# Early couples of an attention and feed-forward kernel: the left-over keys' weights in another place, an earlier step, later squares, and an opening by pairs

## The chip, the cores and the metric

The kernel runs on one core of a Trainium2 chip. The metric is the device time of one execution in microseconds (us). All data is float32.

## The reference

An attention block with normalised queries and keys, followed by a feed-forward block on its output:

```python
# q, k, v: (8 batches, 12 heads, 448 rows, 64)
q_n = q / sqrt(mean(q*q, -1) + 1e-6) * g_q          # k_n likewise with g_k
scores = matmul(q_n, k_n.T) / sqrt(64)
attn = exp(scores - max); attn = attn / (sum(attn) + 1e-9)
x = matmul(attn, v)                                  # as (8*448, 12*64) = (3584, 768)
h = x @ w_in                                         # w_in: 768 x 2048
out = (h * sigmoid(h)) @ w_out                       # w_out: 2048 x 768
```

## The kernel before

**Couples.** The heads are taken in pairs, and two pairs (four heads of one batch) make a couple `c`. There are `NC` = 24 couples, three for each batch. The loop is `visit(c)`, then `between(c)`. Every engine works through its own list in the order in which the Python program issues the instructions (the schedule is manual), so what stands earlier in the program stands earlier in the queue of its engine.

**Scores and weights.** Keys lie on partitions: the 448 keys of a pair are three groups of 128 (`j` = 0, 1, 2) and 64 left over (`j` = `LEFT` = 3). `scores(c, j, i)` makes four matmuls for pair `i` of the couple (L712, eight records in the profile) into one of two `sc` buffers in PSUM, and two exponentials on ScalarE (L717), scaled by the roots of the keys' squares, that write the weights to SBUF. For the left-over keys one call does both pairs, 64 keys each. The weights' places are `e[0]`, `e[1]`, `e[2]` by `j`; in the first six couples (`c < GROUP`) odd couples have `other` in place of `e[0]`. The left-over keys' weights have `eleft`, which is the first half of `e[1]`.

**Weighted sums.** `weigh(c, j, step)` multiplies weights by values (L749) into two banks, `av0` and `av1`, by halves of a key group: half of each for one pair and the other half for the other, and the other way around with the other `step`. Each call for a `j` below `LEFT` needs the weights of both pairs. `turn` (L725) is a one-element copy into such a bank at each change of step; TensorE's next weighted sum waits for it. The sums of couple `c` with `j` = 2 and `LEFT` are made in `visit(c + 1)`, between the next couple's first scores. Then VectorE takes the result out of the banks: in couples 1 to 5 by copies (L1419), later by a division (`divide`, L808).

**Sums over keys.** VectorE adds the weights of `j` = 1 to those of `j` = 0 (`add`, L763), and `sum_up(c)` (L783) sums over keys on TensorE: the weights of `j` = 2, then the added ones, then the left-over ones. VectorE inverts the result (L792), and six DMAs spread it over partitions (L799, L801). `divide` uses that one couple later in the early couples.

**Normalising the next couple.** `normalise(c)` returns four pieces: squares of q for pair 0 and pair 1, squares of k for pair 0 and pair 1. A piece is a square on ScalarE (L467), a reduce on VectorE (L468) and then, at once or for both pairs together, a root: a small scaling on VectorE (L492) and a power on GpSimd (L496). For q the rows are then scaled on GpSimd (L511). `visit` runs the pieces as `beside`, at four points. At the end of a couple `transpose_q` (L629) and `transpose_k` (L647) turn the next couple's rows on TensorE, and ScalarE copies them to `qT` (L633) and `kT` (L649).

**The opening.** Before the loop, couple 0 is normalised by `norm` itself: both pairs' q, then both pairs' k, and couple 0's queries are turned pair by pair (L629, L631). In `visit(0)` couple 1 is normalised by `normalise_alone(1)`, whose squares are on VectorE.

**What else runs early.** The weights `w_in` arrive by DMA in pieces and are opened on ScalarE (L100, L101) and rounded on VectorE and GpSimd (L123 to L134); some sums of them are made on VectorE (L854). From couple 3 on, `fill` deals matmuls of the feed-forward block (L902) between the couples; from couple 6 on they fill TensorE between the attention steps. After the last couple the rest of the feed-forward block follows (L1209).

Of the kernel before, what the change touches and what calls it, by code (L numbers as in the profile page):

```python
# [190 lines left out]
def kernel(  # L191
# [176 lines left out]
    with tc.manual_schedule(), tc.tile_pool(  # L368
# [45 lines left out]
        for i in range(2):  # L414
            norm.squares_q(0, first_q, first_squares[i], i)
            norm.root(0, "q", i)
        for i in range(2):
            norm.squares_k(0, place["k0"], first_squares[i], i)
            norm.root(0, "k", i)
            norm.scale(0, first_q, place["q0"], i, nc.vector)  # L420

    def arm():

        r = copy.copy(room)
        r.w_in = copy.copy(room.w_in)
        state = [dict() for _ in pairs]
        return dict(
            tc=tc, nc=nc, z=z, pairs=pairs, room=r, ring=ring, w_out=w_out, ident=ident,
            minus_half=minus_half, gains=gains, out=out,
            own=dict(  # L430
                NC=NC, loads=loads, place=place, norm=norm, spare=spare, ones=ones, first=first,
                second_q=second_q, squares=squares,
            ),
            plain=(state, lambda n: load_pair(state, n)),
        )
# [100 lines left out]
def bounded(  # L536
# [36 lines left out]
    eleft = e[1][:, 0]  # L573
# [35 lines left out]

    def xT(b, c):  # L610
        return sets[b // 2 % 2].rearrange("p (b c s) -> p b c s", b=2, c=z.NW)[:, b % 2, c, :]
# [7 lines left out]

    def transpose_q(c):  # L620

        t = ps.tile([P, 2, BANK], F32, name="sc", bufs=2)
        both = [t[:, i] for i in range(2)]
        if c == 0:
            both[1] = ps.tile([P, BANK], F32, name="av1")
        for i in range(2):
            for j in range(J):
                rows = q_of(c)[0:R, ts(i * J + j, 2 * D)]
                nc.tensor.transpose(both[i][:, ts(j, R)], rows, ident[0:R, 0:R])  # L629
            if c == 0:  # L630
                (nc.scalar.copy, nc.vector.tensor_copy)[i](qT[:, i], both[i][:, 0:S])  # L631
        if c > 0:
            nc.scalar.copy(qT, t[:, :, 0:S])  # L633
        if GROUP - 2 <= c <= GROUP:
            load_q(c + 2)
        elif c > GROUP + 1:
            load_q(c + 1)
# [65 lines left out]
    def scores(c, j, i=None):  # L703
# [12 lines left out]
        for h in range(2):  # L716
            nc.scalar.activation(  # L717
                eleft[:, h] if j == LEFT else weights(c, j)[:, i, h], two[:, h, 0:S], AF.Exp,
                scale=norm.column(c, i, h, j),
            )  # L720
# [6 lines left out]
    def weigh(c, j, step=0):  # L727
# [6 lines left out]
        for i in order:  # L734
# [5 lines left out]
            for h in range(2):  # L740
                if j == LEFT:
                    v, w = place[f"vleft{c % 2}"][rows, ts(h, D)], eleft[rows, h]
# [11 lines left out]
    def add(c, j):  # L754

        def one(i):
            total = weights(c, 0)[:, i]
            if j == LEFT:
                rows = ds(i * D, D)
                total, more = total[rows], eleft[rows]  # L760
            else:
                more = weights(c, j)[:, i]
# [4 lines left out]
    def sum_up(c):  # L767
# [10 lines left out]
        for k, (which, w) in enumerate(terms):  # L778
            if k == len(terms) - 2:
                yield  # L780
            for h in range(2):
                for i in range(2):
# [3 lines left out]
                        eleft[:, h] if which else w()[:, i, h],  # L786
# [53 lines left out]
    def normalise_alone(c):  # L840

        source = raw_of(c)
        for i in range(2):
            norm.squares_q(c, source, scratch[i], i, True)
            norm.root(c, "q", i)
        norm.squares_k(c, place[f"k{c % 2}"], scratch[0], 0, True)
# [550 lines left out]
    def visit(c):  # L1397

        beside = normalise(c + 1) if 0 < c <= GROUP else []
        if c == GROUP:  # L1400
            beside = beside[2:]
        if c < NC:
            scores(c, 0, 0)
        if c == 0:
            normalise_alone(1)
        run_all(beside[0:1])
# [8 lines left out]
        if c > 0:  # L1415
            weigh(c - 1, LEFT - 1, 1)
            if c - 1 < EARLY:
                for i in range(2):
                    nc.vector.tensor_copy(x_of(c - 1, i), sums[i])  # L1419
                run_all(beside[1:2])  # L1420
# [16 lines left out]
        scores(c, 1, 0)  # L1437
        scores(c, 1, 1)
        if c < GROUP:
            run_all(beside[2:3])  # L1440
        weigh(c, 0, 1)
        scores(c, 2, 0)
# [4 lines left out]
        scores(c, 2, 1)  # L1447
        weigh(c, 0, 0)
        run_all(add(c, 1))
# [3 lines left out]
        scores(c, LEFT)  # L1453
# [80 lines left out]
    transpose_q(0)  # L1534
# [229 lines left out]
```

## Time and profile before

| what | value |
|---|---|
| timed runs | 1325.13 us median of 3 (1323.84 to 1328.43) |
| the profiled execution | 1323.7 us, span 1321.9 us |
| granted TensorE clock, mean | 0.998 |
| TensorE busy | 1298.3 us (98%) |
| VectorE busy | 949.2 us (72%) |
| ScalarE busy | 505.2 us (38%) |
| GpSimd busy | 361.5 us (27%) |
| first scores of couples 0 to 6 | 10.25, 24.25, 40.30, 55.84, 75.98, 97.47, 116.46 us |

How to read it: times in the profile count from the start of the span. PE is TensorE's matmuls, PEld its weight loads, DVE VectorE, ACT ScalarE, POOL GpSimd, SPq the queue that issues most DMAs. A row of the timeline gives start, length, engine, line of the kernel, operation, result and operands; several like instructions that follow each other are merged (`x8`). Brackets give the engine's idle time before the row and who ended it. Ends of matmuls are modelled, so TensorE's starts are read rather than its lengths.

### The profile page before, as it was taken

What the parts mean: (1) busy time and instruction counts of PE and PEld (TensorE: products, weight loads), DVE (VectorE), ACT (ScalarE), POOL (GpSimd) and SP (SyncE); (2) the same over time, 40 slices, a digit from 0 to 9 for tenths busy, and PEclk for the clock granted to TensorE, in tenths of its full rate; (3) what the DMA queues carried; (4) which work ended last, traced back from release to release, by engine and by line L of the source; (5) the groups of instructions that cost most, each with busy time, mean ns of one, the idle gap of its engine ahead of it and who ended that gap; (6) DMA issues with size and microseconds to landing.
All of it is one profiled execution on the core that took longest, in us unless ns stands there. A gap on an engine that the chain in (4) does not pass through costs nothing.

```text
span 1321.9 us, 19806 instructions
## 1 busy us (share of the span) xinstructions
PE 1298.3 (98%) x7193; PEld 829.3 (63%) x7193; DVE 949.2 (72%) x1629; ACT 505.2 (38%) x886; POOL 361.5 (27%) x230
## 2 busy tenths in 40 slices
PE   8989999999999999999999999999999999999998
PEld 4433444444444444444444455558999999999998
DVE  6888776776755555855554686698978787878785
ACT  7966656645545545454444253410100000001000
POOL 6756444343334334333420244410000000000000
PEclk9999999999999999999999999999999999999999
DMA  8674337233443444444321367412323232231411
GB/s 232 169 189 110 113 91 209 80 90 91 95 116 91 97 103 107 96 93 117 81 67 67 106 197 259 150 60 76 100 76 106 76 101 90 92 114 63 132 45 39
DMA packets 249439, 144.94 MB, mean 110 GB/s; under 512 B 184292, under 2 KB 233220, under 8 KB 249332
## 3 DMA queue, kind: packets, MB, share of 16 engines
q1 hardware_dynamic: 248672, 142.42, 38.5%
q8 instruction: 59, 0.97, 0.3%
q0 software_dynamic: 352, 0.96, 0.2%
q14 instruction: 48, 0.39, 0.1%
q10 hardware_dynamic: 308, 0.20, 0.1%
HBM read 93.98 MB, written 41.29 MB: 102 GB/s over the span
## 4 chain that ended last, share of the span: by engine, by line
PE 83%; DVE 6%; ACT 4%; DMA 3%; issue 2%; POOL 1%; SPq 1%; ACTq 0%; DVEq 0%; POOLq 0%
PE mm L902 25%; PE alone L1209 23%; PE mm L1209 8%; PE av L749 8%; PE sc L712 7%; PE alone L902 7%; PE alone L1246 2%; PE sc L783 1%; DMA work<-work 1%; DVE work L763 1%; DVE work L792 1%; ACT work L717 1%; PE mm L1246 1%; ACT stage L1040 1%; DMA hidden<-stage 1%
## 5 line engine op out<-in xcount | busy, mean ns | idle before, releaser
L902 PE MATMUL mm<-x,W 128*128 128x448 f32 x612 | 246.7, 546 | 4.7 <-DVE parts L857 2.0
L717 ACT ACTIVATE work<-sc,rms 128x448 f32<-128x448 f32 x324 | 184.8, 634 | 71.9 <-PE sc L712 58.0
L902 PE MATMUL mm<-sums_x,W 128*128 128x448 f32 x480 | 193.4, 543 | 1.5 <-DVE parts L857 1.5
L902 PEld LDWEIGHTS mm<-x,W 128*128 128x128 f32 x612 | 112.3, 190 | 131.1 <-issue 104.3
L712 PE MATMUL sc<-work 64*64 64x448 f32 x1344 | 165.6, 546 | 1.8 <-ACT work L717 1.5
L763 DVE TENSOR_TENSOR work<-work 128x896 f32<-128x896 f32 (+1 forms) x114 | 123.7, 1118 | 50.1 <-PE av L749 49.6
L749 PE MATMUL av<-work,rows 64*64 64x448 f32 x1296 | 154.1, 543 | 3.3 <-ACT av L725 2.2
L902 PEld LDWEIGHTS mm<-sums_x,W 128*128 128x128 f32 x480 | 89.6, 190 | 95.2 <-issue 85.5
L496 POOL TENSOR_TENSOR rms<-rms,minus_half 128x14 f32<-128x14 f32 (+4 forms) x43 | 105.2, 2449 | 149.2 <-DVE rms L492 139.6
L523 POOL DMA_DIRECT2D out_dram<-x x2 | 1.2, 594 | 443.3 <-DVE x L857 443.3
L1209 PE MATMUL alone<-W,rows 128*128 128x192 f32 x610 | 113.0, 326 | 0.0
L749 PEld LDWEIGHTS av<-work,rows 64*64 64x64 f32 x1296 | 57.8, 132 | 75.7 <-issue 35.8
L1209 PEld LDWEIGHTS alone<-W,rows 128*128 128x128 f32 x610 | 101.5, 190 | 0.0
L712 PEld LDWEIGHTS sc<-work 64*64 64x64 f32 x1344 | 53.6, 133 | 74.8 <-ACT work L717 29.2
L922 POOL TENSOR_TENSOR parts<-parts,stage 128x448 f32<-128x448 f32 x31 | 42.1, 1357 | 148.8 <-DVE parts L857 143.1
L688 POOL TENSOR_TENSOR rms<-rms,minus_half 128x28 f32<-128x28 f32 x12 | 57.5, 4794 | 64.1 <-DVE rms L685 57.4
L1209 PE MATMUL alone<-W,work 128*128 128x192 f32 x382 | 72.2, 326 | 0.0
L1040 ACT ACTIVATE stage<-stage 128x896 f32<-128x896 f32 x63 | 57.3, 945 | 23.6 <-DVE stage L857 22.9
L1219 ACT COPY rows<-alone 128x192 f32<-128x192 f32 x33 | 10.5, 319 | 142.1 <-PE alone L1209 78.4
L468 DVE TENSOR_REDUCE rms<-rows 128x8 f32<-128x512 f32 (+2 forms) x56 | 35.9, 640 | 39.1 <-ACT rows L467 37.9
L1209 PEld LDWEIGHTS alone<-W,work 128*128 128x128 f32 x382 | 63.8, 190 | 0.0
L792 DVE RECIPROCAL work<-sc 128x224 f32<-128x224 f32 x38 | 58.6, 1547 | 5.7 <-PE sc L783 5.5
(250 smaller groups left out, 2114.5 us busy)
## 6 DMA issues: line engine op xcount, KB each, us to landing
hidden<-stage SPq DMA_DIRECT2D x63, 448.0 KB, 3.1
work<-hidden SPq DMA_DIRECT2D x21, 1024.0 KB, 5.1
rows<-in_moe_w_out_dram SPq DMA_DIRECT2D x32, 384.0 KB, 3.4
W<-in_moe_w_in_dram SPq DMA_DIRECT2D x22, 512.0 KB, 5.1
work<-work SPq DMA_DIRECT2D x141, 56.0 KB, 2.0
x<-hidden SPq DMA_DIRECT2D x7, 1024.0 KB, 5.6
rows<-in_q_dram SPq DMA_DIRECT2D x96, 56.0 KB, 2.3
rows<-in_k_dram SPq DMA_DIRECT2D x96, 56.0 KB, 2.3
```

The lines of the kernel that those rows point to most:

```text
L496: nc.gpsimd.tensor_tensor(out=t, in0=t, in1=half, op=ALU.pow)
L688: nc.gpsimd.tensor_tensor(out=f, in0=f, in1=minus_half.to_broadcast([P, n]), op=ALU.pow)
L712: nc.tensor.matmul(two[ds(half * D, D), h, 0:S], keys[rows, ts(half, D)], qT[rows, pair, :], start=True, stop=True,)
L717: nc.scalar.activation(eleft[:, h] if j == LEFT else weights(c, j)[:, i, h], two[:, h, 0:S], AF.Exp, scale=norm.column(c, i, h, j),)
L749: nc.tensor.matmul(sums[i][ds(h * D, D), :], v, w, start=(j == 0 and step == 1), stop=(j == LEFT - 1 and step == 1),)
L763: nc.vector.tensor_tensor(out=total, in0=total, in1=more, op=ALU.add)
L792: nc.vector.reciprocal(out=r[0][:, rows], in_=t[:, rows])
L902: nc.tensor.matmul(t, self.left(name, s), self.right(name, s), start=s == ends[0], stop=s == ends[1])
L922: nc.gpsimd.tensor_tensor(out=u2, in0=u2, in1=p5, op=ALU.add)
L1040: nc.scalar.activation(t, t, AF.Silu)
L1209: nc.tensor.matmul(t, x[:, i], y, start=i == ORDER[0], stop=i == ORDER[-1])
L1246: nc.tensor.matmul(o, a[:, 2 * i + m, t], right_one(name, i)[:, m], start=n == 0, stop=n == len(steps) - 1,)
```

## The change

There are four edits, all in the first seven couples.

1. The left-over keys' weights go to `left_weights(c)`. In couples 0 to 5 that is the second half of the place that the next couple's `j` = 0 weights will have, which the couple before used. From couple 6 on it stays the first half of `e[1]`.
2. In couples 0 to 5 `scores(c, LEFT)` is issued one weighted sum sooner, ahead of `add(c, 1)`, `weigh(c, 1, 0)` and, in couples 0 to 2, ahead of the opening of a weight piece.
3. Couple 4 runs its first piece of `normalise` (q, pair 0) together with the second, behind the copies of the last couple's sums. Couple 6 runs its two k pieces one point later each: the first behind the division, the second behind the scores of `j` = 1.
4. The opening goes pair by pair. k's root of pair 0 comes before q's root of pair 1; the scaling and the transposes of pair 1's queries move into `visit(0)`; and couple 0's scores are made for pair 0 with `j` = 0, 1, 2 and then for pair 1 with `j` = 0, 1, 2, all before the first weighted sum. Couple 1's normalising is split by a `yield` after the first half of its q.

```diff
-        for i in range(2):
-            norm.squares_q(0, first_q, first_squares[i], i)
-            norm.root(0, "q", i)
-        for i in range(2):
-            norm.squares_k(0, place["k0"], first_squares[i], i)
-            norm.root(0, "k", i)
-            norm.scale(0, first_q, place["q0"], i, nc.vector)
+        norm.squares_q(0, first_q, first_squares[0], 0)
+        norm.root(0, "q", 0)
+        norm.squares_q(0, first_q, first_squares[1], 1)
+        norm.squares_k(0, place["k0"], first_squares[0], 0)
+        norm.root(0, "k", 0)
+        norm.root(0, "q", 1)
+        norm.scale(0, first_q, place["q0"], 0, nc.vector)
+        norm.squares_k(0, place["k0"], first_squares[1], 1)
+        norm.root(0, "k", 1)
...
+    def left_weights(c):
+
+        return weights(c + 1, 0)[:, 1] if c < GROUP else e[1][:, 0]
...
+    def first_turn(i):
+
+        if i == 0:
+            t = ps.tile([P, 2, BANK], F32, name="sc", bufs=2)[:, 0]
+        else:
+            t = ps.tile([P, BANK], F32, name="av1")
+        transpose_q_half(0, i, t)
+        (nc.scalar.copy, nc.vector.tensor_copy)[i](qT[:, i], t[:, 0:S])
...
             norm.squares_q(c, source, scratch[i], i, True)
             norm.root(c, "q", i)
+            if i == 0:
+                yield
...
         if c == GROUP:
-            beside = beside[2:]
+            beside = [lambda: None] + beside[2:]
         if c < NC:
             scores(c, 0, 0)
         if c == 0:
-            normalise_alone(1)
-        run_all(beside[0:1])
+            alone = normalise_alone(1)
+            next(alone)
+            scores(c, 1, 0)
+            norm.scale(0, own["first_q"], place["q0"], 1, nc.vector)
+            first_turn(1)
+            run(alone)
+            scores(c, 2, 0)
+        if c != GROUP // 2 + 1:
+            run_all(beside[0:1])
...
-                run_all(beside[1:2])
+                run_all(beside[0 if c == GROUP // 2 + 1 else 1 : 2])
...
-        scores(c, 1, 0)
+        if c > 0:
+            scores(c, 1, 0)
         scores(c, 1, 1)
-        if c < GROUP:
+        if c <= GROUP:
             run_all(beside[2:3])
+        if c == 0:
+            scores(c, 2, 1)
         weigh(c, 0, 1)
-        scores(c, 2, 0)
+        if c > 0:
+            scores(c, 2, 0)
         weigh(c, 1, 1)
         turn(0, nc.scalar.copy)
         if c < GROUP:
             run_all(beside[3:4])
-        scores(c, 2, 1)
+        if c > 0:
+            scores(c, 2, 1)
         weigh(c, 0, 0)
+        if c < GROUP:
+            scores(c, LEFT)
         run_all(add(c, 1))
         weigh(c, 1, 0)
         if c < GROUP // 2:
             room.w_in.open()
-        scores(c, LEFT)
+        if c >= GROUP:
+            scores(c, LEFT)
...
     transpose_k(0)
-    transpose_q(0)
+    first_turn(0)
```

More of the change, by code (lines that the diff above doesn't have):

```diff
@@ L431, in arm @@
                 NC=NC, loads=loads, place=place, norm=norm, spare=spare, ones=ones, first=first,
-                second_q=second_q, squares=squares,
+                first_q=first_q, second_q=second_q, squares=squares,
             ),
@@ L571, in bounded @@
     e = [piece(4 * S).rearrange("p (i h s) -> p i h s", i=2, h=2) for _ in range(3)]
-    eleft = e[1][:, 0]
     r = [piece(S) for _ in range(2)]
@@ L618, in bounded, with transpose_q_half @@
     LEFT = z.KEYS
+    def transpose_q_half(c, i, t):
+        for j in range(J):
+            rows = q_of(c)[0:R, ts(i * J + j, 2 * D)]
+            nc.tensor.transpose(t[:, ts(j, R)], rows, ident[0:R, 0:R])
+    def first_turn(i):
[5 more added lines that the diff above has]
+        (nc.scalar.copy, nc.vector.tensor_copy)[i](qT[:, i], t[:, 0:S])
     def transpose_q(c):
         t = ps.tile([P, 2, BANK], F32, name="sc", bufs=2)
-        both = [t[:, i] for i in range(2)]
-        if c == 0:
-            both[1] = ps.tile([P, BANK], F32, name="av1")
         for i in range(2):
[L627 to L633, printed above, removed]
+            transpose_q_half(c, i, t[:, i])
+        nc.scalar.copy(qT, t[:, :, 0:S])
         if GROUP - 2 <= c <= GROUP:
@@ L717, in scores @@
             nc.scalar.activation(
-                eleft[:, h] if j == LEFT else weights(c, j)[:, i, h], two[:, h, 0:S], AF.Exp,
+                left_weights(c)[:, h] if j == LEFT else weights(c, j)[:, i, h], two[:, h, 0:S], AF.Exp,
                 scale=norm.column(c, i, h, j),
@@ L741, in weigh @@
                 if j == LEFT:
-                    v, w = place[f"vleft{c % 2}"][rows, ts(h, D)], eleft[rows, h]
+                    v, w = place[f"vleft{c % 2}"][rows, ts(h, D)], left_weights(c)[rows, h]
                 else:
@@ L759, in one @@
                 rows = ds(i * D, D)
-                total, more = total[rows], eleft[rows]
+                total, more = total[rows], left_weights(c)[rows]
             else:
@@ L785, in sum_up @@
                         ones[:, which + i if which else 0],
-                        eleft[:, h] if which else w()[:, i, h],
+                        left_weights(c)[:, h] if which else w()[:, i, h],
                         start=(k == 0), stop=(k == len(terms) - 1),
```

## The prediction

> **What bounds the kernel now.** I read the page, then the busy time by stretches, then the timeline of the first 160 us.
>
> ```profile
> PE 1298.3 (98%) x7193; PEld 829.3 (63%) x7193; DVE 949.2 (72%) x1629; ACT 505.2 (38%) x886; POOL 361.5 (27%) x230
> ```
>
> TensorE leaves 23.6 us of the 1321.9 us span. The stretches show where (start:end, length, then busy us of PE, PEld, DVE, ACT, POOL, the granted clock, DMA):
>
> ```profile
> 56.00:76.00 20.00, 17.95 (x161) 7.37 (x157) 15.80 (x23) 14.28 (x27) 13.03 (x8) 1.00 0.55 139
> 76.00:97.00 21.00, 19.63 (x161) 8.30 (x161) 17.24 (x27) 14.56 (x27) 11.85 (x7) 1.00 0.76 193
> ...
> 116.00:126.00 10.00, 7.88 (x58) 2.43 (x56) 9.79 (x18) 6.55 (x14) 6.05 (x5) 0.83 0.37 91
> ```
>
> Couple 3 fills 55.84 to 75.98, couple 4 up to 97.47, and couple 6 begins at 116.46. The diff touches nothing after couple 6. From 155 to 700 us TensorE is busy for 538.63 of 545 us, so what the first 130 us win or lose should reach the end almost whole. In couples 1 and 2 (24 to 56 us) TensorE is busy for 31.77 of 32 us.
>
> The timeline (start, length, engine, line, operation; in brackets the idle time before and who ended it) shows the stalls. In the opening, ScalarE's exponentials:
>
> ```profile
> 11.36 4.55 ACT L717 ACTIVATE work<-sc,rms 128x448 f32<-128x448 f32 x8 [2.02 <-PE sc L712]
> 16.20 1.16 ACT L717 ACTIVATE work<-sc,rms 128x448 f32<-128x448 f32 x2 [0.29 <-PE sc L712]
> 17.25 0.17 ACT L725 COPY av<-minus_half 128x1 f32<-128x1 f32 x1
> ```
>
> In couple 3 the left-over keys' exponential waits until VectorE has read e[1], and TensorE's turn of the next keys waits for that exponential:
>
> ```profile
> 68.56 2.10 DVE L763 TENSOR_TENSOR x<-x,work 128x896 f32<-128x896 f32 x2
> ...
> 69.76 1.16 ACT L717 ACTIVATE work<-sc,rms 128x448 f32<-128x448 f32 x2 [3.69 <-DVE x L763]
> ...
> 70.97 0.98 PE L647 MATMUL sc<-ident,rows 128*128 128x128 f32 x7 [2.05 <-ACT work L717]
> ```
>
> In couple 4 TensorE waits for VectorE's copies of the last couple's sums; after it, GpSimd's last scaling of the next queries:
>
> ```profile
> 81.46 1.15 DVE L1419 COPY x<-av 128x448 f32<-128x448 f32 x2
> ...
> 82.14 1.13 PE L749 MATMUL av<-work,rows 64*64 64x448 f32 x6 [0.66 <-DVE x L1419]
> ```
>
> ```profile
> 86.06 1.04 POOL L511 TENSOR_TENSOR x<-x,rms 112x512 f32<-112x512 f32 x1
> ```
>
> In couple 6 it waits for the fence (L725) that stands behind a square of k on ScalarE, runs slowly after that, and waits again, for the division (L808):
>
> ```profile
> 121.67 1.73 PE L749 MATMUL av<-work,rows 64*64 64x448 f32 x8 [1.97 <-ACT av L725]
> 123.16 2.69 PE L712 MATMUL sc<-work 64*64 64x448 f32 x16
> 126.06 1.12 PE L749 MATMUL av<-work,rows 64*64 64x448 f32 x6 [0.21 <-DVE x L808]
> ```
>
> ```profile
> 125.39 1.15 DVE L808 TENSOR_TENSOR x<-av,work 128x448 f32<-128x448 f32 x2
> ```
>
> **The change part by part.** A step of scores or of a weighted sum takes 0.75 us on a full TensorE (starts at 28.52, 30.02 after two of them); a pair of exponentials takes 1.14 (4.55 / 4).
>
> *Opening.* No arithmetic is added or dropped. VectorE takes one small scaling (0.17) more ahead of the first pair's normalising, which moves from 7.44 to 7.6 and ends at 8.3; transposes and copy follow (8.36, 9.0 to 9.53), and the first scores start at 9.6 instead of 10.25, since the second pair's transposes no longer stand before them. GpSimd has k's root second (7.5 + 1.54 = 9.1), in time. The exponentials start 1.11 later (11.36 - 10.25), at 10.7. But now all six pieces come before any weighted sum, because the first weighted sum needs both pairs. The six end at 10.7 + 6 x 1.14 = 17.6; the last scores start when the fourth piece frees its bank (15.3), then two weighted sums (to 17.7), and the fence copy behind them lets TensorE go on at about 18.2. Before, that was 17.48. The rest of the couple is the same full list as before, so couple 1 begins at 24.25 + 0.7. The second pair's normalising (VectorE, 0.69) waits for the third root on GpSimd, 10.7, and its transposes (0.6) fit in TensorE's holes. Behind it VectorE has couple 1's remaining squares, not needed before 19.9. No DMA changes place in SP's queue. **+0.7 us** at 25 us; bounds -0.65 (first score's lead kept) and +0.8.
>
> *Left-over keys.* The 4 matmuls and 2 exponentials move ahead of one weighted sum and, in couples 0 to 2, of the two opening passes of a weight piece (0.70 + 0.69). In couples 1 and 2 TensorE's own list is full, so the order inside it gives nothing: **0**. The passes now run after the exponential; ScalarE's slack before kT (0.69 idle at 22.72, 0.62 at 38.77, 0.61 at 54.31) covers them; without it 1.4 us a couple. In couple 3 the wait for L763 goes: the exponential can run at 66.3 instead of 69.76 and k's turn at 68.86 instead of 70.97. What is late next is the sum over keys (L783), which needs that same L763, done at 70.66: it ends at 72.2 instead of 73.5, and couple 4's scores start at 74.7, 1.3 earlier. Next, couple 4 runs into VectorE: the division at 75.24 waits 2.19 for a DMA (the spread of couple 2's reciprocals), then a weight rounding to 77.9, the reciprocals 77.84 to 80.80, then the copies. None of that moves by an earlier TensorE. So **0** of the 1.3 is kept by itself.
>
> *Couple 4's q squares later.* The reduce and scaling (0.66 between 80.80 and 81.46) go behind the copies: the weighted sum starts at 81.4 instead of 82.14. What goes with them: two squares on ScalarE (0.63 each) now stand between exponentials, still in time (the fence at about 84.4 against 85.52), no DMA (that load is only made for earlier couples), and on GpSimd two roots (1.64) and two scalings (1.04), which follow the reduce. They start at 82.85 instead of 81.64 and end at 82.85 + 5.4 = 88.3, where 87.1 was the end. TensorE is ready for the second half of those queries at 87.4, so now it waits for GpSimd and has its transposes at 88.85, against 89.08 before: **-0.2**; bounds -1.1 (GpSimd in time) and +2.2 (roots of 2.48 and scalings of 1.48, the longest rows for these shapes).
>
> *Couple 6's k squares later.* The fence then follows the first exponential (119.4), and the next four steps of TensorE end at about 122.0 instead of 125.85. But the next weighted sum still needs the division, and VectorE is busy for 9.79 of 10 us there. The division gains only the one reduce that stood before it (0.68 at 124.80): **-0.6**. The second key group's exponentials are then long done, so the 0.6 us wait for the fence before 129.69 shrinks: **-0.4**. The second k reduce goes behind eight sums of 0.62 and k's root with it, to about 135; it is needed at 156.
>
> Against this stands the clock. The idle 119.6 to 121.7 was followed by half clock:
>
> ```profile
> 122.50:123.00 0.50, 0.50 (x8) 0.18 (x4) 0.50 (x2) 0.50 (x2) 0.38 (x2) 0.50 0.67 155
> ```
>
> The granted clock (0.50 here) came down at about 121.75 and was back by 125.2. That cost nothing before, because TensorE had to wait for the division anyway. Now there is one idle gap from 122.0 to about 125.2, 3.2 us. If the clock falls 2.1 us into it, as it did, and stays down 3.4 us, it covers 2.3 us of the work after the restart, which then takes 1.15 longer: **+1.1**; bounds 0 (couple 3's 2.05 us of idling, with the clock at 1.00 after it) and +1.7 (all 3.4 us at half speed). I take +1.1, since this gap is longer than the one that did bring the clock down.
>
> The Trainium skill, "TensorE: Matmul & The Clock Gate" (Part 1, and the table "Why this matters for your kernels"), says that activity is judged in free-running windows of about 3.4 us and that gaps of over about 3 us should be avoided: a rule against this change. Here 2.1 us were enough once and not enough once. By the rule alone this term would be +1.7, an estimate of mine from that page's half rate over one window, and the sum 0.6 higher.
>
> *Sum.* The opening's +0.7 is carried whole by the full couples 1 and 2. In couples 3 and 4 VectorE's chain hangs on a DMA whose issue moves with the program and whose landing also depends on bytes already queued (DMA share 0.76 there); between 0 and +0.7 I take +0.5, nearer to the program. +0.5 - 0.2 - 0.6 - 0.4 + 1.1 = **+0.4 us**. The profiled execution took 1323.7 us (span 1321.9 and 1.8 around it), so 1324.1. The three timed runs have their median 1.4 higher, but one of them (1323.84) at the profile's level; I stay with it. About 0.3%, 4.0 us, is what a measurement of this kernel can tell from no change.
>
> **The rivals.**
>
> *The stalls are gone for good: faster.* If the spread of the reciprocals lands earlier, because couples 0 to 2 send it off sooner, VectorE's chain moves and TensorE keeps its gaps: 2.05 (couple 3), 0.7 (couple 4), 1.97 and, with the clock staying up, 1.9 (three steps from 121.67 took 4.2, not 2.25), together 6.6; less the opening's 0.7 it is 5.9 faster, 1317.8. For it: each edit sits on a bracketed TensorE wait. Against: 75.24 waits for a DMA, and VectorE has 0.2 us free in 116 to 126.
>
> *GpSimd's chain in couple 4 becomes the bound: slower.* Place: the second half of couple 5's queries. Price: TensorE could start them at 87.4. Each microsecond that GpSimd's last scaling ends after 88.5 (88.3 here) costs one. With the longest rows for these shapes the two roots and scalings take 7.9 instead of 5.4 and end at 90.8, +2.2 on the old time; and since TensorE then idles 3.4 us, the clock comes down for another 3.4 us, +1.7. With the opening's 0.5 and the +0.1 of couple 6 (-0.6 - 0.4 + 1.1) that is +4.5, 1328.2. For it: the same root took 1.64 at 44.12 and 2.48 at 46.98. Against: in this couple both took 1.64.
>
> *It doesn't do what it says.* If the left-over keys' exponential still waits, now for the sums that read the last couple's place, couples 3 and 4 stay as they were: 0.5 - 0.6 - 0.4 + 1.1 = +0.6, 1324.3. That place is read last before 56 us (sum of couple 2), ten before couple 3 writes there, so I give it little.
>
> **How the numbers follow.** My sum 0.55, the faster case 0.27, GpSimd's chain 0.13, no effect 0.05. The sum's unknowns (opening -0.65 to +0.8, couple 4 -1.1 to +2.2, clock 0 to +1.7) put it at some 1321.5 to 1327. Half of the faster case lies below its 1317.8, so the range reaches from 1317.8 to 1328.3 and leaves out some 0.13 below and 0.07 above. Over 0.3% faster: most of the faster case and a little of the sum, 0.27. Slower by that: the larger part of GpSimd's case and a tail of the clock's, 0.13. Same: 0.60.
>
> **What would show it.** Right: first exponential at 10.7, couple 1's first scores near 25.0; no wait for L763 before the left-over exponential of couple 3, and k's turn there near 69; in couple 4 the copies straight after the reciprocals, and TensorE waiting for L511 before the second half of the queries; in couple 6 no wait for L725 after the left-over sums, one gap before the weighted sum that follows L808, and a granted clock of 0.50 behind it. Wrong: couple 1 starting before 24.25; the division by couple 2's sums (75.24) well before 74.5; a clock of 1.00 from 122 to 130.

## The result and the profile after

The changed kernel takes 1326.70 us (median of 20 runs, 1324.08 to 1329.03), the kernel before 1324.11 (20 runs, 1322.69 to 1328.43): the ratio is 1.0017 [1.0010, 1.0023]. Run again later, it took 1325.85 against 1324.62, 1.0006 [0.9997, 1.0014]. By these ratios the change costs 2.3 us (1.3 to 3.0) in the first comparison and 0.8 us (-0.4 to 1.9) in the second; the medians lie 2.6 and 1.2 us apart. The forecast was +0.4, and a gain was given more chance than a loss. The profiled executions differ by more, spans of 1325.8 and 1321.9 us, and the two of them alone mislead: two later kernels whose first five couples are those of before began couple 4 at 77.62 and 81.11 us instead of 75.98, and the changed kernel, profiled again, at 75.79 instead of 77.65.

The page's busy times:

```profile
PE 1299.9 (98%) x7193; PEld 830.4 (63%) x7193; DVE 951.7 (72%) x1629; ACT 505.4 (38%) x886; POOL 362.6 (27%) x230
```

TensorE is busy for 1.6 us longer than before and idle for 2.3 us longer (25.9 against 23.6). The busy time by two stretches around couple 6 (columns as in the prediction):

```profile
116.00:126.00 10.00, 9.41 (x71) 3.90 (x71) 9.78 (x14) 8.65 (x17) 3.50 (x6) 1.00 0.27 65
126.00:155.00 29.00, 26.62 (x122) 13.87 (x123) 26.82 (x39) 13.89 (x23) 16.69 (x10) 0.94 0.38 112
```

The stretch from 116 to 126 us has filled up (9.41 of 10 busy, clock 1.00, against 7.88 and 0.83), and the next one has lost more: the granted clock is 0.94 there and TensorE is busy for 26.62 of 29, where it was 28.58 before. VectorE is busy for 26.82 of those 29 (25.30 before). A part of this is only a shift: couple 6 begins at 119.82 instead of 116.46, so the same point of it comes 3.4 us later in these fixed stretches.

The opening in the timeline of after (start, length, engine, line, operation; in brackets the idle time before):

```profile
10.48 2.21 ACT L729 ACTIVATE work<-sc,rms 128x448 f32<-128x448 f32 x4 [1.19 <-PE sc L724]
11.57 0.69 DVE L513 TENSOR_TENSOR rows<-W,rms 112x512 f32<-112x512 f32 x1 [0.60 <-POOL rms L498]
12.32 0.60 PE L629 MATMUL av<-ident,rows 112*128 112x112 f32 x4 [1.24 <-DVE rows L513]
13.93 4.50 ACT L729 ACTIVATE work<-sc,rms 128x448 f32<-128x448 f32 x8 [1.24 <-PE sc L724]
```

The exponentials start 0.9 earlier than before, but stop for 1.24 us after two of the six pieces: the scores of the third stand in TensorE's list behind the turn of the second pair's queries, and these wait for VectorE, which waits for GpSimd's third root. The six end at 18.43 and couple 1 begins at 25.79.

Couple 3, and the division that waits for the spread reciprocals, in after:

```profile
68.04 1.16 ACT L729 ACTIVATE work<-sc,rms 128x448 f32<-128x448 f32 x2 [0.38 <-PE sc L724]
70.44 0.98 PE L659 MATMUL sc<-ident,rows 128*128 128x128 f32 x7
71.41 2.10 DVE L775 TENSOR_TENSOR x<-x,work 128x896 f32<-128x896 f32 x2
72.55 1.59 PE L795 MATMUL mm<-x,ones 128*32 128x448 f32 x5 [1.12 <-DVE x L775]
78.07 1.16 DVE L820 TENSOR_TENSOR x<-x,work 128x448 f32<-128x448 f32 x2 [2.17 <-DMA work<-work]
```

The left-over exponential (68.04) no longer waits for VectorE, and k's turn follows at once. What is late next is the sum over keys (72.55), and the division still waits 2.17 us for its DMA.

Couple 4:

```profile
83.55 1.09 DVE L1440 COPY x<-av 128x448 f32<-128x448 f32 x2
84.17 1.12 PE L761 MATMUL av<-work,rows 64*64 64x448 f32 x6 [0.97 <-DVE x L1440]
89.94 1.90 POOL L513 TENSOR_TENSOR x<-x,rms 112x512 f32<-112x512 f32 x1
91.90 0.60 PE L629 MATMUL sc<-ident,x 112*128 112x112 f32 x4 [1.12 <-POOL x L513]
```

The copies stand directly behind the reciprocals, and TensorE now waits 1.12 us for GpSimd's last scaling, which took 1.90 us where the same line took 1.04 before.

Couple 6, TensorE's timeline and then half a microsecond behind the gap in the stretches (the granted clock is the seventh figure):

```profile
123.64 1.77 PE L724 MATMUL sc<-work 64*64 64x448 f32 x16
128.38 1.48 PE L761 MATMUL av<-work,rows 64*64 64x448 f32 x6 [2.97 <-DVE x L820]
```

```profile
130.00:130.50 0.50, 0.50 (x8) 0.36 (x4) 0.50 (x1) 0.00 (x0) 0.50 (x1) 0.50 0.83 280
```

The fence's wait is gone, and there is one gap of 2.97 us before the weighted sum behind the division, with half the clock behind it. From that weighted sum to the first feed-forward matmul (136.84) it is 8.5 us; before it was 6.9 (126.06 to 132.93).

### The profile page after: what moved, and what is told of

Same layout as the page of the kernel before. It is cut to its first block, busy times and chain, and to the rows that moved or that the text cites. A ratio compares the mean times of both kernels' runs of the same rounds, so it can differ in the third digit from the quotient of the medians.

```text
span 1325.8 us, 19802 instructions
## 1 busy us (share of the span) xinstructions
PE 1299.9 (98%) x7193; PEld 830.4 (63%) x7193; DVE 951.7 (72%) x1629; ACT 505.4 (38%) x886; POOL 362.6 (27%) x230
## 4 chain that ended last, share of the span: by engine, by line
PE 84%; DVE 5%; ACT 4%; DMA 2%; issue 2%; POOL 1%; SPq 1%; ACTq 0%; DVEq 0%; POOLq 0%
PE mm L916 25%; PE alone L1223 22%; PE av L761 8%; PE mm L1223 8%; PE sc L724 7%; PE alone L916 7%; PE alone L1260 2%; PE sc L795 1%; DVE work L775 1%; DVE work L804 1%; ACT work L729 1%; PE mm L1260 1%; DMA work<-work 1%; ACT stage L1054 1%; DMA hidden<-stage 1%
## 5 line engine op out<-in xcount | busy, mean ns | idle before, releaser
L729 ACT ACTIVATE work<-sc,rms 128x448 f32<-128x448 f32 x318 | 181.2, 634 | 68.6 <-PE sc L724 58.6
L775 DVE TENSOR_TENSOR work<-work 128x896 f32<-128x896 f32 (+1 forms) x114 | 123.7, 1118 | 50.7 <-PE av L761 50.1
L1054 ACT ACTIVATE stage<-stage 128x896 f32<-128x896 f32 x63 | 57.3, 945 | 23.2 <-DVE stage L871 22.4
L470 DVE TENSOR_REDUCE rms<-rows 128x8 f32<-128x512 f32 (+2 forms) x56 | 35.9, 640 | 39.3 <-ACT rows L469 38.1
```

Source lines behind the costliest of these rows:

```text
L729: nc.scalar.activation(left_weights(c)[:, h] if j == LEFT else weights(c, j)[:, i, h], two[:, h, 0:S], AF.Exp, scale=norm.column(c, i, h, j),)
L775: nc.vector.tensor_tensor(out=total, in0=total, in1=more, op=ALU.add)
L1054: nc.scalar.activation(t, t, AF.Silu)
```

## The experiments

All times of a run are compared with the kernel before in the same runs. The edits: O the opening, L the left-over keys, Q couple 4's q, K couple 6's k.

**Each edit by itself.** Four kernels, each the kernel before with one part of the change: L is edits 1 and 2 of the list, O is edit 4, Q and K are the two halves of edit 3.

O alone:

> The kernel before with the opening by pairs alone. Theory (the opening loses, and the full couples 1 and 2 carry the loss whole): ScalarE's first exponential near 10.5 us, but a pause before the third pair of them, the first weighted sum near 17.0, couple 1's first scores near 25.8 instead of 24.25, couple 3's near 57.4, and the time 1.5 to 2.8 us longer than before. Rival (the loss is absorbed in couples 3 and 4, where VectorE waits for a DMA): couple 4's weighted sum within 0.5 us of 82.1, the time at most 0.5 us longer. If the opening were not what costs, couple 1 would begin within 0.3 us of 24.25.

Measured 1325.48 against 1323.58 us, 1.0009 [0.9999, 1.0019]; couple 1 begins at 25.45. In its profile couple 3 begins 1.2 us later than before (57.03 against 55.84), couple 4's weighted sum 0.4 later (82.57 against 82.14) and couple 5 0.4 later (97.91 against 97.47). That is what the rival expected of the profile; the time, with its interval, decides between neither.

L alone:

> The kernel before with the left-over keys' edits alone (their place, and one weighted sum sooner). Theory (couple 3's gain of TensorE is taken back by VectorE's chain, which hangs on a DMA): no wait for L763's successor in couple 3, couple 4's first scores 1.1 to 1.3 us earlier (near 74.8), couple 4's first weighted sum still at 82.1, the time within 0.5 us of before. Rival A (the gain is kept): couple 6 begins 1.3 to 2.1 us earlier, the time 1.3 to 2.1 us shorter. Rival B (this edit is what costs, because the opening of weight pieces comes later on ScalarE): couples 1 and 2 longer by some tenths each, the time 1 us longer.

Measured 1324.16 against 1323.58, 1.0000 [0.9990, 1.0011]. In its profile k's turn in couple 3 stands at 68.90 with no wait before it, and couple 4 begins at 74.47 instead of 75.98. Its couple 6 begins 1.4 us earlier than before (115.05 against 116.46), which is what rival A expected; but the time shows no gain, and in a second profile of the same kernel (further down) couple 6 begins at 116.00.

Q alone:

> The kernel before with couple 4's first q piece moved behind the copies, alone. Theory (GpSimd's second scaling becomes what TensorE waits for): copies near 80.8 and the weighted sum near 81.5 instead of 82.1, but the scaling ends 1.2 to 3 us later than 87.1, TensorE's second half of the next queries waits for it, couple 5 begins 0.3 to 1.5 us later than 97.47, and so does the end. Rival (GpSimd is in time): couple 5 begins 0.6 to 1.1 us earlier, the time shorter by as much.

Measured 1324.82 against 1323.58, 1.0003 [0.9993, 1.0012]. In its profile GpSimd's last scaling took 1.84 us instead of 1.04, and couple 5 begins 22.72 us behind the division by couple 2's sums instead of 22.23.

K alone:

> The kernel before with couple 6's k squares later, alone. Theory (the division frees TensorE 0.6 to 1.0 us sooner, but one long gap takes the place of two and the clock falls behind it): weighted sum near 125.3 instead of 126.06, granted clock 0.50 for some 3.4 us after it, the feed-forward matmuls that began at 132.93 begin 0.3 to 0.9 us later, the time 0 to 0.9 us longer. Rival (the clock stays up, or its fall costs nothing): those matmuls 0.6 to 1.4 us earlier, the time shorter by as much.

Measured 1325.66 against 1323.58, 1.0009 [0.9998, 1.0021]. Its couples 1 to 5 are those of before, and yet couple 4 begins at 81.11: the division by couple 1's sums (65.22) came late and long, the left-over exponential with it (72.42), and TensorE waited:

```profile
73.64 1.76 PE L647 MATMUL sc<-ident,rows 128*128 128x128 f32 x7 [3.77 <-ACT work L717]
```

The granted clock was 0.50 from 72.06 to 78.88 us there, as it was not in before. So one profile of one edit cannot price it at a microsecond, nor do the four intervals alone. What follows takes differences inside a profile that repeat from run to run.

**Each edit left out.** The changed kernel without O, without Q, without K:

> The changed kernel with the old opening. Theory (the opening is one of three costs, about 1 us): couple 1 begins between 24.2 and 25.4 us as with the old opening in the runs so far (24.25, 24.25, 25.18, 25.44), against 25.45 and 25.79 with the new one; the time 0.7 to 1.5 us shorter than the changed kernel, so 0.5 to 1.8 us longer than before. Rival (the opening's loss disappears in couple 3's wait for a DMA): the time as the changed kernel's, 2.2 us longer than before.

> The changed kernel with couple 4's first q piece back in its old place. Theory (that edit costs 0.3 to 1.3 us by GpSimd's later scaling): no wait of TensorE for GpSimd's scaling in couple 4 or a shorter one, copies 0.6 us later behind the reciprocals, the time 0.3 to 1.3 us shorter than the changed kernel. Rival (the edit gains its 0.66): the time 0.3 to 0.7 us longer than the changed kernel.

> All edits but couple 6's later k squares. Theory (couple 6's edit costs 0.5 to 1 through the longer gap and the half clock): the fence's wait of 1.97 in couple 6 is back, couple 6 lasts 38.1 to 38.7, and the time is 0.5 to 1 below the unchanged new kernel, about 1 above before (the opening). Rival (couple 6's edit is neutral, the cost lies in the opening and in couple 4): the time is that of the unchanged new kernel.

Measured: without O 1325.23 against 1324.12, 1.0007 [0.9998, 1.0015]; without Q 1326.44 against 1324.12, 1.0013 [1.0004, 1.0021]; without K 1326.24 against 1324.62, 1.0007 [0.9999, 1.0016]. Leaving out any one of the three leaves the kernel slower than before in the median, but two of the three intervals take in 1, so these runs do not say which edit carries the cost. In the profiles the parts come and go as expected: without O couple 1 begins at 24.25; without Q TensorE no longer waits for GpSimd's scaling in couple 4; without K the fence's wait of 1.97 us is back, but couple 6 lasts 39.79 us, longer than the 38.1 to 38.7 expected. The changed kernel again, in the same runs as the last of them:

> The new kernel unchanged, once more, for comparison in the same runs. All theories: 1326.0 to 1327.0; couple 1 begins between 25.4 and 25.8; the gap before the division in couple 6 is 2.9 to 3.5 us with a granted clock of 0.50 behind it; couple 4 begins anywhere between 75 and 79, because the landing of the spread reciprocals differs between executions of the same code.

1325.85 against 1324.62, as told above; couple 1 at 25.56, couple 4 at 75.79, the gap 3.09 us.

**Couple 6: is the half clock a cost?** In the changed kernel, matmuls that nobody reads are put into the gap. The first attempt wrote into a scores bank:

```diff
+    spot = {}
...
-        two = ps.tile([P, 2, BANK], F32, name="sc", bufs=2)
+        two = spot["t"] = ps.tile([P, 2, BANK], F32, name="sc", bufs=2)
...
             run_all(beside[2:3])
+        if c == GROUP:
+            for _ in range(7):
+                nc.tensor.matmul(
+                    spot["t"][:, 0, S:BANK], ident, ident[:, 0 : BANK - S], start=True, stop=True
+                )
```

> The changed kernel with seven small matmuls more (identity by 64 columns of identity, into unused columns of the scores' bank) in couple 6's gap, behind the scores of the second key group; nothing reads their result. Theory (the clock falls because of the one long gap): the gap shrinks to under 1 us, the granted clock stays at 1.00 through the weighted sum behind the division, the feed-forward matmuls of couple 6 begin 4.5 to 7 us after that weighted sum instead of 8.5, the time 1.2 to 2 us shorter than the changed kernel. Rival (the clock's fall is not what costs): the time as the changed kernel's.

1325.99 against 1324.12, 1.0011 [1.0002, 1.0020]. It tells nothing: the seven waited 1.66 us for the exponentials that read the same bank, and the clock still fell. The second attempt writes into a free bank of the feed-forward products:

```diff
+        if c == GROUP:
+            spot = ps_mm.tile([P, BANK], F32, name="mm")
+            for _ in range(12):
+                nc.tensor.matmul(spot[:, 0:P], ident, ident, start=True, stop=True)
```

> All four edits, and in couple 6 twelve small matmuls (identity by identity, their result is read by nobody) into a free bank of the feed-forward products, issued behind the scores of j = 1, where TensorE otherwise idles for 3.0 to 3.5 us until the division. Unlike in the kernel with seven dummies they wait for nothing on ScalarE. Theory (the half clock behind the gap is a cost of its own): TensorE's gap shrinks below 1 us, the clock stays at 1.00 behind the division, the stretch from that weighted sum to the first feed-forward matmul of couple 6 goes from 8.5 back to 6.9 us, couple 6 lasts 37.2 instead of 38.8, and the time is 1.6 us below that of the unchanged new kernel in the same runs. Rival (VectorE's and GpSimd's lists set the end of couple 6): the clock stays up too, but TensorE then waits for the sums of x (L868) or the added weights, couple 6 lasts 38.5 to 39.3, and the time is within 0.5 of the unchanged new kernel.

1326.38 against 1324.62, 1.0013 [1.0004, 1.0021]. TensorE in this kernel, and the same half microsecond as above:

```profile
123.09 2.94 PE L1466 MATMUL mm<-ident 128*128 128x128 f32 x24
126.33 1.12 PE L761 MATMUL av<-work,rows 64*64 64x448 f32 x6 [0.30 <-DVE x L820]
...
138.65 4.78 PE L916 MATMUL mm<-x,W 128*128 128x448 f32 x12 [0.76 <-DVE parts L871]
143.95 1.02 PE L916 MATMUL mm<-sums_x,W 128*128 128x448 f32 x2 [0.52 <-DVE parts L871]
```

```profile
130.00:130.50 0.50, 0.50 (x10) 0.28 (x12) 0.50 (x1) 0.26 (x1) 0.50 (x1) 1.00 0.22 46
```

The gap is filled, the clock stays at 1.00, and the stretch to the first feed-forward matmul is 6.9 us again (126.33 to 133.20). But TensorE then waits 0.76 and 0.52 us for VectorE's sum of products (`parts`, L871), and couple 6 lasts 39.06 us (117.57 to 156.63) instead of 38.84. So in the changed kernel the half clock had no price, though with little to spare: twelve feed-forward matmuls take 4.53 us by their starts (132.93 to 137.46 in before), so after its 24 TensorE could have gone on at 145.9 in after (136.84 + 2 x 4.53, an estimate), and it went on at 146.00 (below). The same twelve matmuls with L and K alone:

> The kernel before with the left-over keys' edit, couple 6's later k squares and the same twelve matmuls in couple 6; the opening and couple 4 as before. Theory (the edits of couple 6 gain 0.6 and 0.4, and the half clock takes that and more back): with the clock at 1.00 couple 6 lasts 37.7 instead of 38.7, and the time is 1.0 below before, the one version that would beat both. Rival (the sums of x become the bound, as when they were moved): couple 6 lasts 38.7 or more and the time is that of before or up to 1 us more.

1325.01 against 1324.62, 1.0002 [0.9994, 1.0011]; clock 1.00, couple 6 38.89. The version that was to beat both does not.

**What does set the end of couple 6?** In 15 of the 18 profiles VectorE's second sum into `parts`. In the kernel before VectorE has these rows behind the division (the one at 125.39 in the prediction), and TensorE waits for the last of them:

```profile
127.03 1.06 DVE L492 TENSOR_SCALAR rms<-rms 128x14 f32<-128x14 f32 x1
128.66 1.60 DVE L854 TENSOR_TENSOR sums_x<-x,sums_x 128x448 f32<-128x448 f32 x1
...
141.82 0.62 DVE L857 TENSOR_TENSOR parts<-mm,parts 128x448 f32<-128x448 f32 x1
142.50 1.02 PE L902 MATMUL mm<-sums_x,W 128*128 128x448 f32 x2 [0.36 <-DVE parts L857]
```

The same in the changed kernel, and then the division and that sum with the gap filled:

```profile
127.71 1.15 DVE L820 TENSOR_TENSOR x<-av,work 128x448 f32<-128x448 f32 x2
128.77 0.68 DVE L470 TENSOR_REDUCE rms<-rows 128x8 f32<-128x512 f32 x1
129.36 2.09 DVE L868 TENSOR_TENSOR sums_x<-x 128x448 f32<-128x448 f32 x1
131.49 1.60 DVE L868 TENSOR_TENSOR sums_x<-x,sums_x 128x448 f32<-128x448 f32 x1
...
145.32 0.62 DVE L871 TENSOR_TENSOR parts<-mm,parts 128x448 f32<-128x448 f32 x1
146.00 1.02 PE L916 MATMUL mm<-sums_x,W 128*128 128x448 f32 x2
```

```profile
125.66 1.14 DVE L820 TENSOR_TENSOR x<-av,work 128x448 f32<-128x448 f32 x2
143.28 0.62 DVE L871 TENSOR_TENSOR parts<-mm,parts 128x448 f32<-128x448 f32 x1
```

Read the starts. VectorE has no idle time before that sum in any of the 18 profiles, so it comes when VectorE's list is done. From the second `parts` to couple 7's first scores it is 13.35 us before (141.82 to 155.17), 13.34 in after (145.32 to 158.66) and 13.35 with the gap filled. From the division to that `parts` it is 16.43 before, and 17.61 and 17.62 in the other two, with the clock at half and at full. Two more kernels press on this list. In the first, L and K with one step of VectorE's sums (`sum_x`) moved from couple 5's end to behind the division:

```diff
-                sum_x([0, 1], 0)
...
-                    for i in range(1, HW):
+                    for i in range(0 if c == GROUP else 1, HW):
```

> The kernel before with the left-over keys' edits and couple 6's later k squares, and with the first four sums over x (VectorE, 4 x 0.6 us) moved from couple 5's end behind couple 6's division. Theory (VectorE's queue is what the division waits for, so with 2.4 us less ahead of it TensorE's gap goes and the clock stays up): division near 122 to 123 after a couple 6 that begins near 115 to 116.5, gap under 1.5 us, clock 1.00, the time 1.5 to 4 us shorter than before. Rival A (the division waits for the DMA that spreads couple 5's reciprocals): gap and clock as in the changed kernel, the time no shorter than before. Rival B (the sums over x then come too late for the feed-forward matmuls): these wait 1 to 3 us for VectorE, the time as before.

1326.01 against 1324.12, 1.0011 [1.0002, 1.0020]. The division came 6.24 us behind the couple's first scores, 1.9 sooner than in the other profiles with K (mean 8.13), though it now waited 1.22 us for a DMA; the gap shrank to 1.33 us and the clock stayed at 1.00, as the theory had it. But the `parts` came 20.39 us behind the division, the feed-forward matmuls waited 1.24, 2.01 and 0.52 us for VectorE (rival B), and couple 6 lasted 39.97. In the second, the kernel before with two more copies on VectorE behind the division:

```diff
                 divide(c - 1, sums)
+                if c == GROUP:
+                    for i in range(2):
+                        x = x_of(c - 1, i)
+                        nc.vector.tensor_copy(x, x)
```

> The kernel before, and in couple 6 two more copies on VectorE right behind the division (the result of couple 5 onto itself; the values stay as they are). Theory (VectorE's list from the division on sets the end of couple 6; what is moved behind the division, as the changed kernel does with a reduce of k, is paid there): the wait for parts (L857) at 142.5, 0.36 us in the kernel before, grows by most of the copies' length, or further waits for VectorE appear before it, and couple 6 lasts 0.5 to 1.1 longer than its 38.1 to 38.7. Rival (TensorE's own list sets it): couple 6 lasts as long as before, and the time is that of before.

1326.10 against 1325.41, 1.0004 [0.9996, 1.0013]. The expected wait for `parts` did not appear (TensorE was slow itself, behind a gap of 2.04 us), but the list moved as the theory has it:

```profile
126.78 1.15 DVE L808 TENSOR_TENSOR x<-av,work 128x448 f32<-128x448 f32 x2
127.85 3.26 DVE L1431 COPY x<-x 128x448 f32<-128x448 f32 x2
144.51 0.62 DVE L857 TENSOR_TENSOR parts<-mm,parts 128x448 f32<-128x448 f32 x1
```

17.73 us instead of 16.43, then 13.35, and couple 6 lasts 40.14 instead of 38.71. Alone this run does not part the two lists, since by the same estimate TensorE would have been only 0.2 us earlier (140.44 + 4.53, against 145.18); the kernels with the full clock, where TensorE stands and waits for `parts`, do. All profiles together, us from couple 6's first scores to the division, to the second `parts`, to couple 7:

| kernels | to the division | to `parts` | to couple 7 |
|---|---|---|---|
| 8 with K (that with the moved sums left out) | 7.89 to 8.33, mean 8.13 | 17.60 to 17.62, mean 17.61 | 13.33 to 13.36, mean 13.34 |
| 8 without K (that with the added copies left out) | 8.33 to 9.30, mean 8.88 | 16.42 to 16.90, mean 16.59 | 13.34 to 13.73, mean 13.49 |

Two of the eight with K have the gap filled and the full clock, and theirs are the same numbers. In three of the eight without K (without K, Q alone, and the first variant of the opening below) it is 13.73 from `parts` to couple 7: there TensorE, at half clock behind the division, came later than the sum, so the half clock did cost some 0.4 us. K gains 0.75 us ahead of the division, pays 1.0 behind it, and has 0.15 back at the end by not having those three. In the sum couple 6 is 0.1 us longer with it, which is less than the scatter (38.84 to 39.29 with K, 38.09 to 39.79 without).

**The opening.** Two variants of O alone. In the first, a weighted sum is issued between the six pieces:

```diff
+        if c == 0:
+            weigh(c, 0, 1)
         scores(c, 1, 1)
...
-        weigh(c, 0, 1)
         if c > 0:
+            weigh(c, 0, 1)
             scores(c, 2, 0)
```

> The kernel before with the new opening alone, but couple 0's first weighted sum issued right behind the scores of pair 1 with j = 0 instead of behind all six pieces. Theory A (the price of the opening is that all six pieces stand before any weighted sum, so TensorE waits for ScalarE first and has its own work pressed together behind it): the sum fills one of TensorE's waits, couple 1 begins 0.7 earlier than with the new opening as it is, near 24.8 instead of 25.5, and the time falls by as much. Theory B (the price is the 0.9 to 1.2 us hole in the exponentials, before the third piece, where the second pair's turn stands in TensorE's list): couple 1 stays at 25.3 to 25.6.

1327.47 against 1325.41, 1.0014 [1.0006, 1.0023], and couple 1 at 27.41: wrong for both theories. The sum waits for pair 1's first exponentials, and the scores behind it in TensorE's list wait with it; ScalarE's next line reads

```profile
18.20 2.21 ACT L726 ACTIVATE work<-sc,rms 128x448 f32<-128x448 f32 x4 [1.82 <-PE sc L721]
```

The six pieces end at 20.41 and couple 1 begins 7.00 later. In the second, the roots keep their old order:

```diff
+        norm.root(0, "q", 1)
         norm.squares_k(0, place["k0"], first_squares[0], 0)
         norm.root(0, "k", 0)
-        norm.root(0, "q", 1)
```

> The kernel before with the new opening alone, but GpSimd's and VectorE's order of the roots as before (q of both pairs first, then k). Theory A: the first exponential comes back to 11.3, the second pair's turn stands at 9.8, there is no hole, and the six exponential pairs end at 11.3 + 6 x 1.12 = 18.0 instead of 18.1 to 18.4, so that couple 1 begins near 25.2: the hole alone is worth little, because the early start was bought with it. Theory B (the hole is the price): couple 1 begins 0.9 earlier, at 24.6 or sooner.

1326.12 against 1325.41, 1.0005 [0.9995, 1.0015]; couple 1 at 25.30.

```profile
10.59 2.21 ACT L726 ACTIVATE work<-sc,rms 128x448 f32<-128x448 f32 x4 [1.22 <-POOL rms L498]
13.44 4.50 ACT L726 ACTIVATE work<-sc,rms 128x448 f32<-128x448 f32 x8 [0.64 <-PE sc L721]
```

Here the six end at 17.94, and 25.30 is 7.36 later. With O alone they end at 18.09, in after at 18.43, and couple 1 begins at 25.45 and 25.79: 7.36 each time. Over the eight profiles with all six pieces in a row it is 7.32 to 7.39. Couple 1 is the end of the sixth piece plus 7.36. The hole does cost (0.64, 0.86 and 1.24 us in these three), but without it couple 1 would still begin at 24.55 to 24.66, behind the 24.25 of the old opening. That this rest comes from the weighted sums standing behind all six is argued and not shown, since the variant that moved one of them came out later.

**The left-over keys' edit again**, as the one version that might have beaten both:

> The kernel before with the left-over keys' edit alone, a second time, as the one version that may beat both. Theory (the stall of couple 3 is gone, but the division that waits for the spread reciprocals takes it back): the time is that of before within 0.7. Rival (what couple 3 gains is kept): 1.3 below before, with couples 3 and 4 together 40.2 us long, as in the first look, against 41.6 before.

1324.91 against 1325.41, 0.9999 [0.9989, 1.0009]. This is the kernel before within some 1.5 us. Couples 3 and 4 together take 41.2 us in this profile, 40.2 in the first look and 41.6 before, so the rival's number did not come back. No version that was run is faster than the kernel before.

## Why the prediction was wrong, by its own steps

**Opening, +0.7 worked out, +0.5 carried.** The step that failed is "the second pair's normalising waits for the third root, and its transposes fit in TensorE's holes". They did not fit. The third piece's scores stand behind them, and the exponentials stopped for 1.24 us. The third root let VectorE go on at 11.57, where 10.7 was worked out. The rest held: first exponential 10.48 (10.7 was forecast), six pieces of 1.12 us, and 7.36 us from their end to couple 1 (7.35 was implied, 24.95 - 17.6). Seven profiles with O, the two variants left out, begin couple 1 at 25.42 to 26.10, mean 25.65; nine without it at 24.25 to 25.54, mean 24.63. That is +1.0. Four of these sixteen, the latest of their groups, had a granted clock of 0.50 for 3.4 us in the opening (the last section has them); without these four it is 25.58 against 24.26, six profiles each, or +1.3, and couple 3 still begins 1.3 us later (57.16 against 55.84).

How much of it goes on past couple 4 was taken as +0.5 "nearer to the program". The runs lean to more and do not settle it. In 10 of 18 profiles couple 5 begins 21.9 to 22.3 us behind the start of the division by couple 2's sums, before with 22.23 (75.24 to 97.47); in five others, which all have Q, it is 22.7 to 22.8, and in three 23.2 to 24.3, the three with a granted clock of 0.50 for 3.4 or 6.8 us between 72 and 87 us. That division starts at 75.45 in the mean of the nine without O and at 76.34 in the seven with it, +0.9, with about 1.1 us of scatter in each group, so that 0.5 is not excluded. It hangs on a chain in which each link follows the last: in after the division by couple 1's sums (65.40, waiting for its DMA, 2.0 later than before and 2.01 instead of 1.16 us long), the reciprocals (67.33), the two DMA issues (70.32 and 75.43), the division (78.07). In before the same five stand at 63.40, 64.48, 67.47, 72.60 and 75.24. From the reciprocals to the division it is 10.74 and 10.76 us. So in this pair the DMA chain carries the delay and does not swallow it. Over all 18 profiles that stretch takes 9.69 to 11.34 us, and the division starts at 73.8 to 78.1.

**Left-over keys, 0.** Right as far as the runs can tell, and with the waits that it named. The stall of couple 3 is gone, couple 4 begins at 74.47 and 74.72 with L alone (75.98 before; 74.7 was forecast), and the division that waits for the DMA takes it back: couple 5 follows it by 22.23 and 22.24 us in the two profiles of L alone. The division itself came earlier in both (73.83 and 74.77 against 75.24), but three other kernels with L and the old opening have it at 74.47 to 76.15, so whether L moves it at all is lost in the scatter. Two timed comparisons give 1.0000 and 0.9999, each good to about 1.4 us.

**Couple 4, -0.2.** The copies' gain came as forecast: from the reciprocals to the weighted sum 3.50 us (80.67 to 84.17) instead of 4.30. The mis-sized term is GpSimd's last scaling, 1.90 us instead of the 1.04 taken from before, now beside VectorE's additions (L775, 88.86 to 90.95): TensorE waited 1.12 us. From the division to couple 5 it is 22.76 us in after instead of 22.23, +0.5; over the seven profiles with Q the mean is 22.5, +0.3. In five of the seven GpSimd's scaling took 1.84 to 1.93 us and couple 5 came 22.7 to 22.8 behind the division; in the other two it took 1.04 and 1.10, and couple 5 came 21.9 behind it, a gain of 0.3, close to the forecast. The upper bound (+2.2) covered the +0.5, the value taken did not. (The 89.08 given there for the transposes before is no row: the eight began at 88.16, and the next matmul at 88.98.)

**Couple 6, -0.6 - 0.4 + 1.1 = +0.1.** The size was right by luck and the mechanism wrong. The gap and the half clock came as described (2.97 us, 0.50 from 129.0 to 132.4), and the weighted sums behind it took 1.6 us longer. But the changed kernel without the half clock is no faster, so the +1.1 was not paid. The step that failed is "-0.4" and with it "+1.1": both looked at TensorE's and ScalarE's lists behind the division only. VectorE's own list there, one reduce longer and with two slow sums (2.09 and 1.60 us, where before one took 1.60 and the small scaling 1.06), ends 1.2 us later, and that list sets couple 7. What should have stood there is -0.75 ahead of the division, and +1.0 and -0.15 behind it. The Trainium skill, "TensorE: Matmul & The Clock Gate" (Part 1, and the table "Why this matters for your kernels"), has activity windows of about 3.4 us and counsels against idle gaps over about 3 us. The gap of 2.97 us here was followed by one stretch of 3.4 us at half clock, and filling it gained nothing.

**Sum.** The means over the profiles give +0.9 (opening, at the division) + 0 + 0.3 + 0.1 = 1.3 us; the timed runs gave 2.3 and 0.8. The forecast's +0.4 missed by the opening's hole, which is shown at couple 1, by GpSimd's scaling, and by how much of the hole is carried to the end, which the runs leave uncertain by about 0.5 us. The pair of profiles that showed +3.9 adds the luck of the DMA chain: couple 3 +1.54, the division by couple 2's sums +2.83, couple 5 +3.36, couple 7 +3.49.

**The rivals.** The stalls are gone in couples 3 and 6, and no time with them. GpSimd's chain in couple 4 did become what TensorE waits for, at +0.5 us where the rival had +2.2. That the change does nothing is excluded by couple 3.

What stays open: the timed price of each single edit, since every interval of an edit alone takes in 1, and why the spread reciprocals land at different times in executions of the same code (the division that waits for them stands at 78.07 and at 75.30 in the two profiles of the changed kernel).

## What to carry to other kernels

A stall that is taken away gives time only if nothing else ends at the same place a moment later: look for the instruction from which the next stage starts at a constant distance (here 13.35 us behind one VectorE addition in 15 of 18 profiles, 7.36 behind the sixth piece of exponentials in all eight that have them in a row), and price each edit by what it does to that instruction. When small operations are moved to the other side of the step that was late, add them up again on that side, on every engine's list. And before a difference of one microsecond is read from two profiles, look at a third of the same code.

## What the runs showed of the hardware

- The granted clock fell to 0.50 for 3.4 us at a time in couple 6 (129.0 to 132.4 in after), for twice that with Q alone (123.0 to 129.8). Of 15 profiles with an unfilled gap of 1.97 us or more in that couple, 12 show it; the two of L alone (gaps of 1.97 and 1.31, and of 1.97 and 2.03 us) and the one with the moved sums (2.01) do not. In the kernel with the seven small matmuls a gap of 1.66 us was followed by it.
- The same opening code begins couple 1 at 24.25 to 24.27 us in six profiles and at 25.18, 25.44 and 25.54 in three. These three had a granted clock of 0.50 in the opening (10.62 to 14.03, 10.37 to 13.78 and 9.60 to 13.01 us), the six had not. Of the profiles with the new opening the one without K had it (9.44 to 12.85), and it begins couple 1 last of the seven, at 26.10.
- Where VectorE and GpSimd work side by side, operations of one or both take longer: a sum of 128x448 took 2.09 us instead of 0.61 beside a GpSimd scaling (128.93, 2.04 for two), two copies of that size 3.26 (beside two such scalings, there at 127.42), a division 2.01 instead of 1.16 (beside the scaling at 65.85). In couple 4 with Q GpSimd's scaling took 1.84 to 1.93 us instead of 1.04 in five profiles; in the other two it took 1.04 and 1.10, and the VectorE addition beside it 1.95 and 1.93 instead of 1.08.
